# Casts ahead of the power, stores on GpSimd's queue, and the eleventh pair turned by DMA, in a fused windowed-attention and gMLP kernel

## The chip, the core and the metric

The kernel runs on one core of a Trainium2 chip. A core has five engines that run at the same time, each with its own list of instructions in a fixed order, and they wait for each other on semaphores: TensorE (PE in the profile; matmuls, with its weight loads shown as PEld), VectorE (DVE), ScalarE (ACT), GpSimd (POOL) and SyncE (SP, which here only issues transfers). Transfers are moved by 16 DMA engines. An engine that issues a transfer puts it on its own queue and goes on; the transfer lands some microseconds later. The metric is the time of one execution on the device in microseconds; lower is better.

## The reference

There are 4 batches, 8 heads, 768 tokens and 64 channels per head. Attention sees a window of 128 tokens and 4 sink tokens at the start; a gated MLP block (gMLP) follows, with a matrix that mixes tokens.

```python
def _attn_ref(q, k, v, n_sink, window):
    scores = np.matmul(q, k.transpose(0, 1, 3, 2)) / np.sqrt(D)
    rel = pos[:, None] - pos[None, :]
    keep = (pos[None, :] < n_sink) | ((rel >= 0) & (rel < window))
    scores = np.where(keep, scores, -1e9)
    a = np.exp(scores - np.max(scores, axis=-1, keepdims=True))
    a = a / (np.sum(a, axis=-1, keepdims=True) + 1e-09)
    return np.matmul(a, v)

def _moe_ref(x, w_in, g_ln, w_sg, b_sg, w_out):
    h = gelu_tanh(x @ w_in)
    u, v = h[..., :512], h[..., 512:]
    v_n = (v - mean(v)) / np.sqrt(var(v) + 1e-06) * g_ln
    v_s = np.einsum('ts,bsd->btd', w_sg, v_n) + b_sg[None, :, None]
    return x + (u * v_s) @ w_out

# x is the attention's output, all heads side by side: 4 x 768 x 512
```

## The kernel before

**Pairs and batches.** The work is cut into 16 pairs of heads, numbered 0 to 15, four to a batch (batch b holds pairs 4b to 4b + 3). The 768 tokens are 6 tiles of 128. Keys and queries of a pair are loaded in f32 (`load`, L91), cast to bf16 (`cast`, L102, on GpSimd for all but the first pair), and turned so that channels lie on the partitions. There are two ways to turn them. `columns` (L217) does six 128x128 transposes on TensorE into a PSUM bank, which ScalarE or VectorE copies out. `columns_by_dma` (L230) issues one transposing DMA for k and one for q on SyncE's queue. The two ways need different orders of the tokens, so the load differs too: up to pair `FIRST` - 1 a partition takes six neighbouring tokens, a run of 1,536 bytes; from `FIRST` on (L89; `in_rows`) it takes one token of each tile, in rows of 256 bytes. v is always loaded in rows. `FIRST` is 11, so pairs 11 to 15 are turned by DMA.

**One pair.** `score` (L253) computes the scores in three groups of up to 1,024 columns; ScalarE takes their exponentials (L283). `keep_band` (L285) zeroes what lies outside the window: group 0 on VectorE with a mask (L292), groups 1 and 2 on GpSimd with two selects each (L300, L302). `values` (L309) multiplies with v in two halves and VectorE divides by the sums (L334, L335). `turn_x` (L339, TensorE) or `turn_x_by_dma` (L354, SyncE's queue) turns the result for the MLP.

**One batch of the MLP.** `hidden` (L587) has 14 units on TensorE: six for v (L372, L379), each followed by a gelu on ScalarE and statistics on VectorE (L383, L384), and eight for u (L391). After the eighth unit `inverse_root` (L402) forms 1/sqrt(var + 1e-6): VectorE adds (L406, tile w) and GpSimd takes the power (L407, tile y). VectorE then normalises six tiles (L413, tile vn). `spatial` (L417) mixes the tokens in eight groups of six matmuls (L423), each closed by two instructions of VectorE (L426, L429). `project` (L449) makes one tile of 128 output rows: four matmuls (L455), then either VectorE adds x (L465), or, with `by_act`, a fifth matmul adds x (L458) and ScalarE copies (L463); then the tile is stored (L467). Spatial groups and projections wait in a list, `fillers`, and are run between the steps of the next batch's attention.

**The order is written out by hand** in `ORDER` (L719) and `INSIDE` (L714: steps put behind a unit of `hidden`), and each engine's list follows it. The words: `S n g` scores, `m n g` masks, `A0 n`, `A1 n` the two halves of the values, `ck`, `cq`, `cv n` casts on GpSimd, `KA`, `QA` turn k or q with ScalarE's copy, `QV` with VectorE's, `TD n` turn k and q by DMA, `XV n`, `XD n` turn x with VectorE's copy or by DMA, `L n` load k and q of pair n and v of pair n - 1, `F c` run c fillers, `B b` the hidden layer of batch b. SyncE's queue holds loads, turns by DMA and most stores, and an instruction that waits there holds all behind it.

**Buffers that make waits.** A loaded tile of each of k, q and v has three buffers (`loads`, L55), the cast tile two (L107), so a cast of pair n waits until pair n - 2 has been turned; turned tiles have three (L222). PSUM has four single banks in turn for all but scores (`bank`, L211), and two double banks for scores.

At the end (L783 on) the last pair's values, the last hidden layer and its spatial groups and projections run. Its six tiles are stored as `rows` (L606) and `project_last` (L431), which stores one half from SyncE and one from ScalarE. Before that, `count_good` (L479) counts on GpSimd whether all sums are in range; if not, a general path runs, which these inputs do not take.

Of the kernel before, what the change touches and what calls it, by code (L numbers as in the profile page):

```python
# [18 lines left out]
def kernel(  # L19
# [14 lines left out]
    nc = tc.nc  # L34
    V, G, A = nc.vector, nc.gpsimd, nc.scalar

    B, H, S, Dh = q.shape
# [6 lines left out]
    HP = H // 2  # L44
# [3 lines left out]
    HT = NT // 2  # L48
# [37 lines left out]

        nc.sync.dma_start(out=gates[:, i, :], in_=behind)

    FIRST = 3 * HP - 1  # L89

    def load(n, which, eng=None, in_rows=False):  # L91
        b, hp = divmod(n, HP)
        src = dict(k=k, q=q, v=v)[which]
        dst = loads.tile([128, 2, NT, 64], F32, name=which + "_sb")
        order = "h (t p) d -> p h t d" if which == "v" or in_rows else "h (p t) d -> p h t d"
        (eng or nc.sync).dma_start(
            out=dst, in_=src[b, 2 * hp:2 * hp + 2].rearrange(order, t=NT))
        raw[n, which] = dst
# [12 lines left out]
    def load_all(n):  # L111

        for which, m in (("k", n), ("q", n), ("v", n - 1)):
            if m < NP:
                load(m, which, in_rows=m >= FIRST)

# [94 lines left out]
    def bank(shape, dtype, name):  # L211
        return ps_m.tile(shape, dtype, name=name, tag="m")
# [162 lines left out]
    def hidden_v(b, j):  # L375
        if (b, j) not in hvs:
            open_v(b, j)
        h_ps, c = hvs.pop((b, j)), KD - 1
        nc.tensor.matmul(h_ps, xT[b][:, c, 128 * j:128 * (j + 1)],  # L379
                         w_in_sb[:, c, DF:], start=False, stop=True)  # L380
        A.activation(out=v_alls[b][:, j, :], in_=h_ps, func=AF.Gelu_apprx_tanh)  # L381
        st = small.tile([128, 6], F32, name="st")
        V.bn_stats(out=st, in_=v_alls[b][:, j, :])  # L383
        V.bn_aggr(out=mvs[b][:, j, :], in_=st)  # L384

    def hidden_u(b, f, n):
        if f == 0 and n == 0:
            uTs[b] = work.tile([128, KU, S], BF16, name="uT", bufs=1)
        h_ps = bank([128, 512], F32, "hu")
        for c in range(KD):  # L390
            nc.tensor.matmul(h_ps[:, 0:NH], w_in_sb[:, c, 128 * f:128 * (f + 1)],  # L391
                             xT[b][:, c, NH * n:NH * (n + 1)],
                             start=(c == 0), stop=(c == KD - 1))
        A.activation(out=uTs[b][:, f, NH * n:NH * (n + 1)],  # L394
                     in_=h_ps[:, 0:NH], func=AF.Gelu_apprx_tanh)
# [6 lines left out]
    def inverse_root(b):  # L402

        w = small.tile([128, NT], F32, name="w", bufs=2)
        y = small.tile([128, NT], F32, name="y", bufs=2)
        V.tensor_scalar(out=w, in0=mvs[b][:, :, 1], scalar1=1e-6, scalar2=None, op0=ALU.add)  # L406
        G.tensor_tensor(out=y, in0=w, in1=minus_half, op=ALU.pow)  # L407
        rstds[b] = y

    def normalise(b, j):  # L410
        if j == 0:
            vns[b] = work.tile([128, NT, DF], BF16, name="vn", bufs=1)
        V.tensor_scalar(out=vns[b][:, j, :], in0=v_alls[b][:, j, :],  # L413
                        scalar1=mvs[b][:, j, 0:1], scalar2=rstds[b][:, j:j + 1],
                        op0=ALU.subtract, op1=ALU.mult)

    def spatial(b, f, n):  # L417
        if f == 0 and n == 0:
            gTs[b] = work.tile([128, KU, S], BF16, name="gT", bufs=1)
        cols = slice(NH * n, NH * (n + 1))  # L420
        vs = bank([128, 512], F32, "vs")
        for si in range(NT):
            nc.tensor.matmul(vs[:, 0:NH], vns[b][:, si, 128 * f:128 * (f + 1)],  # L423
                             wsgT[:, si, cols], start=(si == 0), stop=(si == NT - 1))
        gv = small.tile([128, NH], BF16, name="gv")
        V.scalar_tensor_tensor(  # L426
            out=gv, in0=vs[:, 0:NH], scalar=g_sb[:, f:f + 1], in1=b_bc[:, cols],
            op0=ALU.mult, op1=ALU.add)
        V.tensor_mul(gTs[b][:, f, cols], gv, uTs[b][:, f, cols])  # L429
# [19 lines left out]
    def project(b, t, by_act, ends=None, store=nc.sync):  # L449

        rows = slice(128 * t, 128 * (t + 1))
        o_ps = bank([128, 512], F32, "o_ps")
        o_sb = small.tile([128, DM], F32, name="o_sb", bufs=6)
        for c in range(KU):
            nc.tensor.matmul(o_ps, gTs[b][:, c, rows], w_out_sb[:, c, :],  # L455
                             start=(c == 0), stop=(c == KU - 1 and not by_act))
        if by_act:
            nc.tensor.matmul(o_ps.rearrange("p (h d) -> p h d", h=HP), iden, x_sb[b][:, :, t, :],  # L458
                             start=False, stop=True)

        def end():
            if by_act:
                A.copy(o_sb, o_ps)  # L463
            else:
                V.tensor_add(o_sb.rearrange("p (h d) -> p h d", h=HP),  # L465
                             o_ps.rearrange("p (h d) -> p h d", h=HP), x_sb[b][:, :, t, :])
            store.dma_start(out=out[b, rows, :], in_=o_sb)  # L467

        if ends is None:
            end()  # L470
        else:
            ends.append(end)
# [34 lines left out]
    def general():  # L507
# [15 lines left out]
        for b in range(B):  # L523
            begin_x(b)
            for hp in range(HP):
                n = HP * b + hp
                for which in "kqv":
                    load(n, which)
                for which in "kqv":
                    cast(n, which, V)  # L530
                columns(n, "k", A)
                columns(n, "q", V)
                for i in range(NT):
                    for l in range(2):
                        stable(n, i, l, m[min(i, 2)], low[:, min(i, 2), :])
                turn_x(n, V)
            hidden(b, {})
            fill(len(fillers))
# [41 lines left out]
    fillers = []  # L580
# [6 lines left out]
    def hidden(b, between):  # L587
        units = [lambda j=j: hidden_v(b, j) for j in range(NT)]
        units += [lambda f=f, n=n: hidden_u(b, f, n) for n in range(2) for f in range(KU)]
        after = {NT + 1: [lambda: inverse_root(b)]}  # L590
        for j in range(NT):
            after.setdefault(NT + 1 + j, []).append(lambda j=j: normalise(b, j))
        for i, unit in enumerate(units):
            unit()
            for step in after.get(i, []) + between.get(i, []):
                step()
        gate = [[lambda f=f, n=n: spatial(b, f, n) for f in range(KU)] for n in range(2)]
        if b < B - 1:
            fillers.extend(gate[0] + gate[1])
            by_act = (1,)  # L600
            order = (0, 2, 4, 1, 3, 5) if b < B - 2 else (1, 0, 2, 3, 4, 5)
            fillers.extend(lambda ends=None, t=t: project(b, t, t in by_act, ends) for t in order)
            return


        rows = [lambda t=t: project(b, t, t in (0, 4), store=nc.sync if t else G)  # L606
                for t in range(NT - 1)]
        fillers.extend(gate[0] + [gate[1][0], rows[0], gate[1][1], gate[1][2], rows[1],
                                  gate[1][3]] + rows[2:])
        fillers.append(lambda: project_last(b, NT - 1))  # L610
# [85 lines left out]
    for j in range(3):  # L696
# [15 lines left out]

    LAST = NT + 2 * KU - 1
    INSIDE = {  # L714
        1: {1: "A0 8", 3: "A1 8", 5: "KA 9", 6: "L 12", 7: "QA 9",
            9: "XD 8, ck 11, cq 11, TD 11, L 13", LAST: "cv 10, S 9 0 1, F 1, QV 10, F 1"},
        2: {1: "A0 12", 3: "A1 12", 6: "L 15, L 16", 9: "XD 12", LAST: "S 13 0 1, F 2"},
    }
    ORDER = """  # L719
        S 4 0 1, W 3 4 5, m 4 0 1, F 1, KA 5, QV 5, F 1, S 4 2, m 4 2, ck 6, cq 6, cv 5, F 1,  # L720
        L 8, S 5 0 1, A0 4, m 5 0 1, F 1, KA 6, S 5 2, m 5 2, A1 4, F 1, QA 6,
        ck 7, cq 7, cv 6, F 1, XV 4,
        L 9, S 6 0 1, A0 5, m 6 0 1, F 1, KA 7, S 6 2, m 6 2, A1 5, F 1, QA 7,
        ck 8, cq 8, cv 7, F 1, XV 5,
# [1 line left out]
        ck 9, cq 9, cv 8, F 1, XV 6,  # L726
        L 11, S 8 0 1, A0 7, m 8 1, D, S 8 2, m 8 2, A1 7, E, m 8 0, ck 10, cq 10, cv 9,
        O 1 0, O 1 1, XV 7, O 1 2, B 1,
        m 9 0 1, F 1, KA 10, F 1, S 9 2, m 9 2, ck 12, cq 12, TD 12, F 1,
        S 10 0 1, A0 9, m 10 0 1, F 1, S 10 2, m 10 2, A1 9, XD 9, L 14,  # L730
        F 1, cv 11, ck 13, cq 13, TD 13, F 1,
        S 11 0 1, A0 10, m 11 0 1, F 1, S 11 2, m 11 2, A1 10, F 1, cv 12, ck 14, cq 14, TD 14,
        F 1, XV 10,
        S 12 0 1, A0 11, m 12 1, F 1, S 12 2, m 12 2, A1 11, F 1, m 12 0, cv 13, F 1,
        O 2 0, O 2 1, XV 11, O 2 2, B 2,
        ck 15, m 13 0 1, cq 15, F 2, S 13 2, m 13 2, TD 15, cv 14, F 1,
        S 14 0 1, A0 13, m 14 0 1, F 1, S 14 2, m 14 2, A1 13, XD 13, F 1, cv 15, F 1,
        S 15 0 1, A0 14, m 15 0 1, F 1, S 15 2, m 15 2, A1 14, XD 14, F 1, G, F 1
    """
# [1 line left out]
    ends = []  # L741
# [97 lines left out]
```

## Time and profile before

| | us |
|---|---|
| median of 3 runs | 164.02 (163.75 to 164.38) |
| the profiled execution | 164.03 |
| its span, from the first instruction to the last | 162.0 |

| engine | busy us | share of the span |
|---|---|---|
| TensorE, matmuls | 150.3 | 93% |
| VectorE | 128.8 | 79% |
| ScalarE | 103.0 | 64% |
| GpSimd | 87.2 | 54% |

The span is some 2 us shorter than the execution's time; a difference between two kernels can be read in either. The granted clock of TensorE is full (1.00) in all stretches that are shown. Times in the profile's rows are microseconds from the start of the span. A row of a timeline has the start, the length, the engine, the line, the operation, what it writes and reads, and how many instructions are merged; in brackets stands idle time ahead of it and what ended it. Lengths of matmuls are modelled and overlap, so the step from one start to the next is what a group of them costs. A few records of matmuls are missing, so that a group of four may read x3.

### The profile page before, as it was taken

To read this page: it belongs to the slowest core of one execution; us is meant where nothing else is said; L and a number is where in the kernel's file an instruction comes from. 1 tells how busy PE (TensorE), PEld (TensorE's weight loads), DVE (VectorE), ACT (ScalarE), POOL (GpSimd) and SP (SyncE) were. 2 spreads that over 40 slices of the span, in tenths; PEclk is the share of its full clock that TensorE was granted. 3 is DMA by queue.
4 is the path that set the end of the run, shared out by engine and by line. 5 is a ranking of instruction groups with operands and counts; after the bars stand their busy time and mean duration, and the time that the engine had idled before them with its cause. 6 is when DMAs were issued, how large, how long until landed. Compare 5 with 4: busy or idle time off the path is not lost.

```text
span 162.0 us, 4332 instructions
## 1 busy us (share of the span) xinstructions
PE 150.3 (93%) x1713; PEld 89.9 (55%) x1731; DVE 128.8 (79%) x279; ACT 103.0 (64%) x139; POOL 87.2 (54%) x121
## 2 busy tenths in 40 slices
PE   2999999999999999999899999999999899999940
PEld 2546574566667675565556655565566445555420
DVE  6786985966899995796999994969999957797820
ACT  3179978789777699788865576679659157401020
POOL 6567680434899989708449997031997221101000
PEclk9999999999999999999999999999999999999995
DMA  4999979999999999999897999999626420050352
GB/s 129 339 337 264 210 103 272 222 254 318 305 232 321 260 304 314 234 256 171 182 249 175 154 220 126 304 236 200 178 52 53 134 109 4 0 194 0 129 202 75
DMA packets 65090, 31.68 MB, mean 196 GB/s; under 512 B 53829, under 2 KB 62041, under 8 KB 65065
## 3 DMA queue, kind: packets, MB, share of 16 engines
q1 hardware_dynamic: 61616, 27.80, 74.8%
q0 software_dynamic: 3024, 3.03, 11.0%
q10 hardware_dynamic: 424, 0.53, 1.0%
q8 instruction: 15, 0.25, 0.7%
q14 instruction: 11, 0.08, 0.1%
HBM read 24.81 MB, written 6.29 MB: 192 GB/s over the span
## 4 chain that ended last, share of the span: by engine, by line
PE 45%; DVE 23%; issue 11%; POOL 10%; DMA 3%; ACT 3%; SPq 1%; POOLq 0%; ACTq 0%; DVEq 0%
PE vs L423 9%; PE hu L391 7%; PE o_ps L455 6%; PE hv L372 5%; DVE gv L426 4%; DVE gT L429 4%; DVE vn L413 4%; PE sc L269 3%; PE av L326 3%; DMA q_sb<-in_q_dram 3%; ACT ex L283 2%; DVE x L335 2%; POOL ex L300 2%; POOL ex L302 2%; PE kps L221 2%
## 5 line engine op out<-in xcount | busy, mean ns | idle before, releaser
L283 ACT ACTIVATE ex<-sc 128x1024 bf16<-128x1024 f32 x48 | 47.5, 1024 | 15.3 <-PE sc L269 6.4
L423 PE MATMUL vs<-wsgT,vn 128*128 128x384 bf16 x192 | 35.3, 326 | 0.5 <-DVE qT L227 0.4
L423 PEld LDWEIGHTS <-vn 128*128 128x128 bf16 x192 | 17.9, 98 | 11.3 <-issue 0.5
L300 POOL TENSOR_SCALAR_AFFINE_SELECT ex<-ex 128x512 bf16<-128x512 bf16 x24 | 18.6, 773 | 10.4 <-ACT ex L283 10.4
L455 PE MATMUL o_ps<-w_out_sb,gT 128*128 128x512 bf16 x83 | 22.2, 379 | 0.9 <-DVE x L335 0.4
L391 PE MATMUL hu<-xT,w_in_sb 128*128 128x384 bf16 x128 | 22.4, 326 | 0.0
L426 DVE SCALAR_TENSOR_TENSOR gv<-vs,g_sb,b_bc 128x384 bf16<-128x384 f32 x32 | 19.5, 610 | 2.1 <-PE vs L423 1.4
L381 ACT ACTIVATE v_all<-hv 128x512 f32<-128x512 f32 x24 | 13.3, 599 | 9.6 <-PE hv L379 8.4
L383 DVE BATCH_NORM_STATS2 st<-v_all 128x6 f32<-128x512 f32 x24 | 16.1, 670 | 3.5 <-ACT v_all L381 3.5
L335 DVE TENSOR_TENSOR x<-av,rcps 128x384 bf16<-128x384 f32 x32 | 17.8, 557 | 1.1
L372 PE MATMUL hv<-w_in_sb,xT 128*128 128x512 bf16 x68 | 18.4, 379 | 0.3
L394 ACT ACTIVATE uT<-hu 128x384 bf16<-128x384 f32 x32 | 15.7, 493 | 4.3 <-PE hu L391 3.8
L108 POOL CAST k_bf<-k_sb 128x768 bf16<-128x768 f32 x15 | 12.7, 845 | 10.3 <-DMA k_sb<-in_k_dram 10.3
L413 DVE TENSOR_SCALAR vn<-v_all,mv,y 128x512 bf16<-128x512 f32 x24 | 13.3, 619 | 5.9 <-POOL y L407 5.9
L429 DVE TENSOR_TENSOR gT<-gv,uT 128x384 bf16<-128x384 bf16 x32 | 15.5, 484 | 1.9
L108 POOL CAST q_bf<-q_sb 128x768 bf16<-128x768 f32 x15 | 14.7, 981 | 3.3 <-DMA q_sb<-in_q_dram 2.4
L391 PEld LDWEIGHTS <-w_in_sb 128*128 128x128 bf16 x128 | 12.1, 98 | 7.7
L269 PE MATMUL sc<-qT,kT 64*128 64x256 bf16 (+2 forms) x384 | 16.0, 256 | 0.4
L407 POOL TENSOR_TENSOR y<-w,minus_half 128x6 f32<-128x6 f32 x4 | 5.4, 1345 | 20.0 <-DVE w L406 20.0
L326 PE MATMUL av<-v_sb,ex 128*128 128x65 bf16 x352 | 16.1, 194 | 0.0
L326 PEld LDWEIGHTS <-ex 128*128 128x128 bf16 x352 | 13.0, 97 | 4.9 <-issue 1.7
L105 POOL CAST v_sb<-v_sb 128x768 bf16<-128x768 f32 x16 | 13.7, 855 | 3.4 <-DMA v_sb<-in_v_dram 3.3
(89 smaller groups left out, 216.5 us busy)
## 6 DMA issues: line engine op xcount, KB each, us to landing
k_sb<-in_k_dram SPq DMA_DIRECT2D x16, 384.0 KB, 6.9
v_sb<-in_v_dram SPq DMA_DIRECT2D x16, 384.0 KB, 6.4
q_sb<-in_q_dram SPq DMA_DIRECT2D x15, 384.0 KB, 6.9
out_dram<-o_sb SPq DMA_DIRECT2D x22, 256.0 KB, 2.6
wsg_sb<-in_moe_w_sg_dram POOLq DMA_DIRECT2D x2, 576.0 KB, 11.4
w_in_sb<-in_moe_w_in_dram POOLq DMA_DIRECT2D x2, 256.0 KB, 5.8
w_in_sb<-in_moe_w_in_dram POOLq DMA_DIRECT2D x1, 512.0 KB, 6.7
w_out_sb<-in_moe_w_out_dram POOLq DMA_DIRECT2D x1, 512.0 KB, 9.5
```

Source lines behind the costliest of these rows:

```text
L108: eng.tensor_copy(dst.rearrange("p t (h d) -> p h t d", h=2), src)
L269: nc.tensor.matmul(sc[part, 512 * l + w:512 * l + w + n_q], kT[rows, 128 * j + wide * a:128 * j + wide * (a + 1)], qT[rows, 128 * j:128 * ...
L283: A.activation(out=exps[n][:, g, :], in_=sc, func=AF.Exp, scale=scale)
L300: eng.affine_select(out=diag, in_=diag, compare_op=ALU.is_ge, fill=0.0, base=0, pattern=[[0, 2], [0, 2], [1, 128]], channel_multiplier=-1)
L326: nc.tensor.matmul(av[:, m, l, :], probs(j, l, half), v_sb[:, l, j, :], start=first, stop=False)
L335: V.tensor_mul(x_sb[b][:, hp, HT * c:HT * (c + 1), :].rearrange("p i (l d) -> p i l d", l=2), av[:, :, :, 0:64], rcp.to_broadcast([128, HT ...
L372: nc.tensor.matmul(hvs[b, j], xT[b][:, c, 128 * j:128 * (j + 1)], w_in_sb[:, c, DF:], start=(c == 0), stop=False)
L391: nc.tensor.matmul(h_ps[:, 0:NH], w_in_sb[:, c, 128 * f:128 * (f + 1)], xT[b][:, c, NH * n:NH * (n + 1)], start=(c == 0), stop=(c == KD - 1))
L423: nc.tensor.matmul(vs[:, 0:NH], vns[b][:, si, 128 * f:128 * (f + 1)], wsgT[:, si, cols], start=(si == 0), stop=(si == NT - 1))
L426: V.scalar_tensor_tensor(out=gv, in0=vs[:, 0:NH], scalar=g_sb[:, f:f + 1], in1=b_bc[:, cols], op0=ALU.mult, op1=ALU.add)
L429: V.tensor_mul(gTs[b][:, f, cols], gv, uTs[b][:, f, cols])
L455: nc.tensor.matmul(o_ps, gTs[b][:, c, rows], w_out_sb[:, c, :], start=(c == 0), stop=(c == KU - 1 and not by_act))
```

## The change

- `FIRST` is 10 instead of 11: k and q of pair 10 are loaded in rows and turned by DMA (`TD 10`); `KA 10` and `QV 10` are gone.
- Behind unit 6 of the hidden layer of batch 1 now stand `TD 10, L 12, ck 11, cq 11`; the casts stood behind unit 9, so that on GpSimd they came after the power (L407), which is issued behind unit 7. `cv 10` moves from the end of that hidden layer to behind the masks of pair 9.
- `L 13`, `L 14`, `L 15` and `L 16` stand behind `TD 12`, `TD 13`, `TD 14` and `TD 15`. Before, they were issued behind units 9 and 6 of the hidden layers of batches 1 and 2 or ahead of the turn of the pair before.
- The casts and turns of pairs 13 and 14 stand later: those of 13 behind the masks of pair 11, those of 14 behind the masks of pair 12. `cq 15` stands ahead of the masks of pair 13.
- `KA 6` stands behind `S 5 2`.
- Tile 5 of batch 1 is added to x on TensorE and copied by ScalarE (`by_act`) instead of added by VectorE.
- Five of the six stores of batch 2 (tiles 0, 2, 3, 4, 5) are issued from GpSimd's queue instead of SyncE's. In batch 3 GpSimd stores tile 3 instead of tile 0.

```diff
-    FIRST = 3 * HP - 1
+    FIRST = 3 * HP - 2
...
-            by_act = (1,)
+            by_act = (1, 5) if b == B - 3 else (1,)
             order = (0, 2, 4, 1, 3, 5) if b < B - 2 else (1, 0, 2, 3, 4, 5)
-            fillers.extend(lambda ends=None, t=t: project(b, t, t in by_act, ends) for t in order)
+
+            by_pool = () if b < B - 2 else order[1:]
+            fillers.extend(lambda ends=None, t=t: project(b, t, t in by_act, ends,
+                                                          G if t in by_pool else nc.sync)
+                           for t in order)
...
-        rows = [lambda t=t: project(b, t, t in (0, 4), store=nc.sync if t else G)
+        rows = [lambda t=t: project(b, t, t in (0, 4), store=G if t == HT else nc.sync)
...
-        1: {1: "A0 8", 3: "A1 8", 5: "KA 9", 6: "L 12", 7: "QA 9",
-            9: "XD 8, ck 11, cq 11, TD 11, L 13", LAST: "cv 10, S 9 0 1, F 1, QV 10, F 1"},
-        2: {1: "A0 12", 3: "A1 12", 6: "L 15, L 16", 9: "XD 12", LAST: "S 13 0 1, F 2"},
+        1: {1: "A0 8", 3: "A1 8", 5: "KA 9", 6: "TD 10, L 12, ck 11, cq 11", 7: "QA 9",
+            9: "XD 8, TD 11", LAST: "S 9 0 1, F 2"},
+        2: {1: "A0 12", 3: "A1 12", 9: "XD 12", LAST: "S 13 0 1, F 2"},
...
-        L 8, S 5 0 1, A0 4, m 5 0 1, F 1, KA 6, S 5 2, m 5 2, A1 4, F 1, QA 6,
+        L 8, S 5 0 1, A0 4, m 5 0 1, F 1, S 5 2, m 5 2, KA 6, A1 4, F 1, QA 6,
...
-        m 9 0 1, F 1, KA 10, F 1, S 9 2, m 9 2, ck 12, cq 12, TD 12, F 1,
-        S 10 0 1, A0 9, m 10 0 1, F 1, S 10 2, m 10 2, A1 9, XD 9, L 14,
-        F 1, cv 11, ck 13, cq 13, TD 13, F 1,
-        S 11 0 1, A0 10, m 11 0 1, F 1, S 11 2, m 11 2, A1 10, F 1, cv 12, ck 14, cq 14, TD 14,
+        m 9 0 1, F 2, S 9 2, m 9 2, ck 12, cq 12, TD 12, L 13, cv 10, F 1,
+        S 10 0 1, A0 9, m 10 0 1, F 1, S 10 2, m 10 2, A1 9, XD 9,
+        F 1, cv 11, F 1,
+        S 11 0 1, A0 10, m 11 0 1, F 1, S 11 2, m 11 2, A1 10, F 1, ck 13, cq 13, TD 13, L 14, cv 12,
         F 1, XV 10,
-        S 12 0 1, A0 11, m 12 1, F 1, S 12 2, m 12 2, A1 11, F 1, m 12 0, cv 13, F 1,
+        S 12 0 1, A0 11, m 12 1, F 1, S 12 2, m 12 2, A1 11, F 1, m 12 0, ck 14, cq 14, TD 14, L 15, cv 13, F 1,
         O 2 0, O 2 1, XV 11, O 2 2, B 2,
-        ck 15, m 13 0 1, cq 15, F 2, S 13 2, m 13 2, TD 15, cv 14, F 1,
+        ck 15, cq 15, TD 15, L 16, m 13 0 1, F 2, S 13 2, m 13 2, cv 14, F 1,
```

## The prediction

> **What bounds the kernel now.** I read the page first (busy shares), then who waited for whom on TensorE, then TensorE's own timeline around the eleventh pair.
>
> ```profile
> span 162.0 us, 4332 instructions
> ## 1 busy us (share of the span) xinstructions
> PE 150.3 (93%) x1713; PEld 89.9 (55%) x1731; DVE 128.8 (79%) x279; ACT 103.0 (64%) x139; POOL 87.2 (54%) x121
> ```
> ```profile
> PE o_ps L455 <- DVE x L335: 0.4, 1, 0.4
> PE vs L423 <- DVE qT L227: 0.4, 1, 0.4
> ```
>
> TensorE is busy for 93% of the span, and these two waits are all that the view of waits lists for it after its warm-up, apart from one of 0.2 us in the start. So the time is the length of TensorE's list of work. Whatever leaves that list is gained, whatever makes TensorE wait is lost, and what happens on another engine counts only when TensorE comes to need it. Here is the list where the eleventh pair (number 10 in the code) is turned:
>
> ```profile
> 75.88 0.61 PE L269 MATMUL sc<-qT,kT 64*128 64x256 bf16 x8
> 76.42 1.04 PE L455 MATMUL o_ps<-w_out_sb,gT 128*128 128x512 bf16 x3
> 77.30 0.50 PE L221 MATMUL qps<-iden,q_bf 128*128 128x128 bf16 x6
> 77.63 1.03 PE L455 MATMUL o_ps<-w_out_sb,gT 128*128 128x512 bf16 x4
> 78.50 1.14 PE L423 MATMUL vs<-wsgT,vn 128*128 128x384 bf16 x6
> 79.70 0.50 PE L221 MATMUL kps<-iden,k_bf 128*128 128x128 bf16 x6
> 80.56 1.14 PE L423 MATMUL vs<-wsgT,vn 128*128 128x384 bf16 x6 [0.37 <-DVE qT L227]
> 81.63 0.36 PE L269 MATMUL sc<-qT,kT 64*32 64x256 bf16 x16
> ```
>
> The columns are start, length and instruction. Lengths of matmuls overlap, so I take steps from start to start.
>
> **The change part by part.** *Pair 10 by DMA.* The two groups of six transposes (L221) leave TensorE, and their copies leave VectorE and ScalarE. From the scores at 75.88 to the next at 81.63 are 5.75 us. Without the groups there remain 0.54 (scores), 0.88 and 0.87 (two projections) and two spatial groups of 1.07 each (80.56 to 81.63): 4.43 us. That is a gain of 1.3 us. The groups alone would be 0.33 each (77.30 to 77.63), 0.66 together; the rest is the wait for the copy of qT. So the bounds are 0.66 and 1.3. I take 1.3, because the spatial sums need only the normalised rows (vn), and those come earlier:
>
> ```profile
> 73.34 1.34 POOL L407 TENSOR_TENSOR y<-w,minus_half 128x6 f32<-128x6 f32 x1 [5.34 <-DVE w L406]
> 74.66 0.81 POOL L108 CAST k_bf<-k_sb 128x768 bf16<-128x768 f32 x1
> 75.42 1.02 POOL L108 CAST q_bf<-q_sb 128x768 bf16<-128x768 f32 x1
> 76.39 1.02 POOL L105 CAST v_sb<-v_sb 128x768 bf16<-128x768 f32 x1
> ```
> ```profile
> 74.00:80.00 6.00, 4.33 (x6) 1.00 0.90 157
> 108.00:113.00 5.00, 3.31 (x6) 1.00 1.37 219
> 139.00:143.00 4.00, 2.40 (x6) 1.00 0.03 12
> ```
>
> The second view is VectorE's time on line 413 in three stretches, six instructions each. Beside the three casts above six take 4.33 us; in batch 2, with one such cast beside them, 3.31; in batch 3, with GpSimd idle, 2.40. *The casts ahead of the power* move two of the three in front of y, and cv 10 goes behind the masks. So vn should end 74.7 + 2.4 to 3.3 = 77.1 to 78.0, and TensorE asks for the sixth only at about 78.17 + 5/6 of 1.07 = 79.1.
>
> What the power waits for is new: in GpSimd's order it now stands behind cq 11, which needs the buffer that QA 9 reads:
>
> ```profile
> 71.55 0.50 PE L221 MATMUL qps<-iden,q_bf 128*128 128x128 bf16 x6
> ```
>
> That ends at 72.05; a cast of 0.81 to 1.02 ends at 72.9 to 73.1, and y starts at 73.34 anyway. I cost it at nothing. The cover is 0.3 us here and 1.1 to 2.0 us ahead of the sixth vn. The Trainium skill, page "SBUF — State Buffer", section "Who interferes with whom", says that a VectorE instruction with at most one SBUF input outside the 2-port modes does not contend with GpSimd. The casts now run beside statistics (L383) of that kind, so by that rule they keep 0.81 us, the power is not late, and the rival below that makes it late gets less; no run here shows it yet.
>
> *Rows instead of runs for k and q of pair 10* (FIRST one lower). The two transfers are 2 x 384 KB. A stretch with mostly long runs and one with short rows show what the DMA engines then move (last column, GB/s):
>
> ```profile
> 50.00:51.20 1.20, 1.20 (x21) 0.82 (x18) 1.20 (x2) 1.13 (x2) 1.20 (x2) 1.00 1.06 359
> 105.00:111.00 6.00, 6.00 (x41) 3.35 (x41) 4.38 (x12) 4.82 (x10) 2.10 (x2) 1.00 1.30 224
> ```
>
> 786 kB take 2.2 us at 359 and 3.5 at 224, so all that is queued behind lands some 1.3 us later, and the two new turns add themselves. Behind them on SyncE's queue stand L 12's three loads, XD 8 and TD 11. Their first user is the scores of pair 11, ahead of which TensorE still has all of pair 10's scores and values and four more spatial groups to do, so I cost this at nothing; without that cover it is 1.3 us.
>
> *Loads timed anew.* L 13, L 14 and L 15 now stand behind the turn of the pair before them, which waits for GpSimd's casts, and XD 9 stands behind L 13. Durations on that queue:
>
> ```profile
> 85.34 1.22 SPq L235 DMA_TRANSPOSE kT<-k_bf  x1
> 86.66 1.22 SPq L235 DMA_TRANSPOSE qT<-q_bf  x1
> 87.98 1.25 SPq L356 DMA_TRANSPOSE xT<-x  x1
> 89.28 1.43 SPq L96 DMA_DIRECT2D k_sb<-in_k_dram  x1
> 90.77 0.70 SPq L96 DMA_DIRECT2D q_sb<-in_q_dram  x1
> 91.51 1.67 SPq L96 DMA_DIRECT2D v_sb<-in_v_dram  x1
> 93.35 2.51 SPq L235 DMA_TRANSPOSE kT<-k_bf  x1
> ```
> ```profile
> 97.96 1.24 PE L372 MATMUL hv<-w_in_sb,xT 128*128 128x512 bf16 x5
> ```
> ```profile
> DMA to landing us min/median/max: 4.1/4.5/5.0
> ```
>
> The turn of pair 12 begins 3.7 us after S 9 2 (81.63 to 85.34: exponential, masks, cast k). S 9 2 comes at 80.3 now, so the turn at 84.0; its two issues take 2.6 and L 13's three 4.1 (89.28 to 93.35), so XD 9 is issued at 90.7 and lands, by the row for xT, 4.1 to 5.0 us later: 94.8 to 95.7. The hidden layer that reads it comes at 97.96 - 1.3 = 96.6. A margin of 1 to 2 us, where before it was 97.96 - (87.98 + 5.0) = 5. Landing like a plain load in a full queue (6.9, below) it would be 1.0 late. I charge 0.2 us for this and the other late users, between 0 and 2.
>
> *One projection of batch 1 to ScalarE* adds a matmul of 128x512 to TensorE's list: 0.87 / 4 = +0.2 us. VectorE loses an addition there, besides the copy of qT and about 0.9 us on vn of batch 2 (3.31 to 2.40) if its casts wait for their loads. That matters where VectorE was late for TensorE:
>
> ```profile
> 126.32 1.04 PE L455 MATMUL o_ps<-w_out_sb,gT 128*128 128x512 bf16 x4 [0.44 <-DVE x L335]
> ```
>
> I take 0.4 for it; 0 if VectorE is no earlier.
>
> *Stores.* Five of batch 2 go to GpSimd's queue: two before the counting, three after the last power, where it has nothing else to do, so they cost nothing; if they held the last power, TensorE would wait for vn of batch 3 by as much. In the last batch tile 3 goes to GpSimd and tile 0 to SyncE. The end:
>
> ```profile
> 155.53 1.12 SPq L467 DMA_DIRECT2D out_dram<-o_sb  x1
> ...
> 156.30 0.38 ACTq L447 DMA_DIRECT2D out_dram<-o_last  x1
> 156.74 0.54 SPq L447 DMA_DIRECT2D out_dram<-o_last  x1
> ```
>
> SyncE's last store stands behind one that took 1.12 us to issue. With one less ahead it can go earlier, but the end gains at most the 0.44 to ScalarE's last. I take 0.2, between 0 and 0.4. The Trainium skill speaks against this part: "SBUF — State Buffer", section "A bandwidth-pool intuition that's wrong", has a store from GpSimd's queue taking 3.1 us instead of 0.62 beside a VectorE copy, as its descriptors cannot be written; by that this term would be 0 and the sum 162.7. No run here shows it. KA 6 behind S 5 2 is the same work in another order, covered by those scores: nothing.
>
> Sum from the profiled execution's 164.03 (the median shown is 164.02): - 1.3 + 0.2 - 0.4 - 0.2 + 0.2 = 162.5.
>
> **The rivals.** *The loads come late (slower).* One ring: turn of q, then k and q of the next load, then casts, then the next turn. One lap is 1.3 (86.66 to 87.98) + 1.5 (k's issue, 89.28 to 90.77) + the landing L + 1.0 (cast) = 3.8 + L. cq 12 ends at about 85.3 (84.0 + 1.3, where its own turn follows it); three laps and XD 9 later cq 15 ends at 98.0 + 3 L, and it now stands ahead of the masks that A0 13 needs:
>
> ```profile
> 116.02 0.48 PE L326 MATMUL av<-v_sb,ex 128*128 128x65 bf16 x10
> ```
> ```profile
> 90.77 4.40 DMA q_sb<-in_q_dram
> ```
> ```profile
> q_sb<-in_q_dram SPq DMA_DIRECT2D x15, 384.0 KB, 6.9
> ```
>
> A0 13 comes at 116.02 - 1.1 = 114.9, less 0.8 for the first mask: it holds up to L = 5.4. Each us more costs 3. The chain of waits shows 4.40 in this very stage, the page's median is 6.9 (most of those loads met a full queue). At 5.9 the gain is gone, at 6.9 the time is 167.1.
>
> *Only the bare work goes (no change by measure).* The waits return at other places because VectorE stays as late: - 0.66 + 0.2 = 163.6. For it: VectorE is busy 79% of the span, more than any engine but TensorE, and both waits above name it. Against it: between the second power and the hidden layer of batch 2 it sheds more than TensorE does (a copy, and up to 1.9 of the 4.33 us on vn).
>
> *The power is late.* If q of pair 11 lands after 72.1, cq 11 and y slide, and past the 1.1 to 2.0 us of cover TensorE stands before the spatial sums. 2 us late would leave 164.03 - 0.5 = 163.5. Against it: in its old place at 75.42 the cast of q 11 waited for nothing, so the load had landed some time before; how long, this trace's rows do not say.
>
> **How the numbers follow.** Forecast 0.64, late loads 0.17, bare work 0.13, late power 0.06. Below 163.2 is faster by more than 0.5%, which is about what a measurement can tell: the forecast gives 0.64 and the late loads with a small L 0.04, so 0.68. Above 164.8 lies the rest of the late loads, 0.13; between them the bare work and the late power, 0.19. The range: all terms at their good ends give 162.5 - 0.2 - 0.2 = 162.1, and I go 0.8 below it, to 161.3, for waits that hide in the steps of matmuls and may go too (78.50 to 79.70 is 0.13 longer than 1.07, and no wait is shown there). The upper end takes L = 6.1: 164.6.
>
> **What would show it.** Right: no L221 of pair 10 on TensorE; six vn after the second power in 2.4 to 3.3 us; S 9 2 at 80.3; the hidden layer of batch 2 at 96.6; no wait at the projection after A0 15. Wrong: a wait of TensorE for xT at the hidden layer of batch 2, GpSimd idle for q_sb ahead of cq 14 or cq 15 with ScalarE's exponentials done, y of batch 1 starting later than 73.4, or of batch 2 behind cv 13.

## The result and the profile after

| | before | changed |
|---|---|---|
| median of the runs | 164.19 us (6 runs) | 162.64 us (161.87 to 165.96, 6 runs) |
| ratio to before | 1 | 0.9885, 95% interval 0.9853 to 0.9917 |
| ratio, the same kernel in a second set of runs | 1 | 0.9898, interval 0.9849 to 0.9946 |
| profiled execution, span | 164.03, 162.0 us | 161.53, 159.7 us |

By the ratio the change makes the kernel 1.2% faster, some 1.9 us. Every kernel here has now and then an execution that is some per cent longer, which counts in the medians of this document but not in its ratios; the first profiled execution of the change (165.42 us) was such a one, so the lines here are of another profiled execution of the same kernel, run repeat. What the first one lost is shown at the end. The page of the second and its view of waits (engine, line, tile, who was waited for, and us in total, times, longest):

```profile
span 159.7 us, 4312 instructions
## 1 busy us (share of the span) xinstructions
PE 149.1 (93%) x1702; PEld 89.4 (56%) x1720; DVE 126.1 (79%) x277; ACT 102.8 (64%) x139; POOL 89.3 (56%) x126
```
```profile
...
PE xps L343 <- DVE x L335: 0.2, 1, 0.2
```

TensorE is still the bound, with 1.2 us less work. The two waits of 0.4 us are gone, and a new one of 0.2 us stands at `XV 10`, for VectorE's x; the lines left out are waits in the kernel's first 40 us. TensorE's timeline around pair 10, and at the two hidden layers behind it:

```profile
75.81 0.61 PE L269 MATMUL sc<-qT,kT 64*128 64x256 bf16 x8
76.35 1.90 PE L455 MATMUL o_ps<-w_out_sb,gT 128*128 128x512 bf16 x7
78.09 2.11 PE L423 MATMUL vs<-wsgT,vn 128*128 128x384 bf16 x12
80.13 0.36 PE L269 MATMUL sc<-qT,kT 64*32 64x256 bf16 x16
```
```profile
96.69 1.46 PE L372 MATMUL hv<-w_in_sb,xT 128*128 128x512 bf16 x6
...
126.12 1.03 PE L455 MATMUL o_ps<-w_out_sb,gT 128*128 128x512 bf16 x4
126.98 0.81 PE L372 MATMUL hv<-w_in_sb,xT 128*128 128x512 bf16 x3
```

Between the scores at 75.81 and S 9 2 at 80.13 there are 4.32 us instead of 5.75, and no L221 stands between them. The hidden layer of batch 2 comes at 96.69. VectorE's time on vn (line 413; columns: window, its length, busy time and count, clock, DMA share, GB/s):

```profile
74.00:80.00 6.00, 2.83 (x6) 1.00 1.34 226
106.00:112.00 6.00, 3.33 (x6) 1.00 1.22 227
136.00:142.00 6.00, 2.88 (x6) 1.00 0.02 8
```

The group of batch 1 takes 2.83 us instead of 4.33; that of batch 2 is as long as before (3.31). In batch 3 GpSimd is idle, and there six take 2.88, before and after. The prediction has 2.40 for them: its window began at 139.00, after the first of the six, which begins at 138.52. In batch 0 of the kernel before, GpSimd idle too, six take 2.83. So 2.83 us is all that the casts could leave, and each cast that runs beside the six adds some 0.5 us: 2.83 with none, 3.31 with one, 3.82 with two (run casts_behind), 4.33 with three. GpSimd around the second power, and where the loads come latest:

```profile
70.46 0.83 POOL L108 CAST k_bf<-k_sb 128x768 bf16<-128x768 f32 x1 [2.55 <-PE kps L221]
72.10 0.83 POOL L108 CAST q_bf<-q_sb 128x768 bf16<-128x768 f32 x1 [0.81 <-PE qps L221]
73.26 1.34 POOL L407 TENSOR_TENSOR y<-w,minus_half 128x6 f32<-128x6 f32 x1 [0.34 <-DVE w L406]
...
110.11 0.89 POOL L108 CAST k_bf<-k_sb 128x768 bf16<-128x768 f32 x1 [2.20 <-DMA k_sb<-in_k_dram]
111.93 1.24 POOL L108 CAST q_bf<-q_sb 128x768 bf16<-128x768 f32 x1 [0.93 <-DMA q_sb<-in_q_dram]
113.12 0.77 POOL L300 TENSOR_SCALAR_AFFINE_SELECT ex<-ex 128x512 bf16<-128x512 bf16 x1
```

The power starts at 73.26, having waited 0.34 us for w alone: it was not late. cq 15 did wait for its load, the masks of pair 13 stand right behind it without a gap, and they start at 113.12.

Starts of such rows give a table of stages for every run below, in us: A from the scores of S 9 to S 9 2, B from there to the hidden layer of batch 2, C from S 13 to the hidden layer of batch 3, D from there to the end of the span. Between B and C lie 11.76 or 11.77 us in every run. A row is one profiled execution, that of the change its second.

| run | A | B | C | D | ratio to before, interval |
|---|---|---|---|---|---|
| before | 5.75 | 16.33 | 18.87 | 33.41 | 1 |
| the change | 4.32 | 16.56 | 18.53 | 32.72 | 0.9898 (0.9849 to 0.9946) |
| no_turn10 | 4.99 | 16.57 | 18.47 | 33.08 | 0.9925 (0.9889 to 0.9961) |
| casts_behind | 4.33 | 17.54 | 18.48 | 33.03 | 0.9945 (0.9906 to 0.9985) |
| loads_early | 4.32 | 17.13 | 19.21 | 33.21 | 0.9939 (0.9906 to 0.9972) |
| casts_loads | 4.32 | 18.18 | 19.20 | 33.27 | 0.9983 (0.9954 to 1.0011) |
| turn10_only | 4.46 | 20.16 | 18.87 | 33.13 | 1.0053 (1.0012 to 1.0094) |
| loads_only | 5.75 | 17.16 | 19.35 | 33.50 | 1.0054 (1.0026 to 1.0082) |
| stores_sp | 4.32 | 16.56 | 18.48 | 33.06 | 0.9867 (0.9839 to 0.9895) |
| act_one | 4.32 | 16.56 | 18.25 | 32.98 | 0.9865 (0.9806 to 0.9923) |
| ka6_back | 4.32 | 16.57 | 19.96 | 32.98 | 0.985 (0.982 to 0.9881) |
| three_parts | 4.33 | 16.57 | 18.66 | 33.02 | 0.9901 (0.9863 to 0.9939) |
| turn9 | 5.56 | 17.54 | 19.61 | 34.00 | 1.0049 (1.0019 to 1.0079) |

How far can such a row be trusted? The change's first profile has A 4.33, B 16.56, C 18.47 and D 33.01. In the five runs whose edit touches neither the turn of pair 10 nor its casts nor the loads, A and B agree with that within 0.01. So a few tenths in A and B are the edit's, also where the ratios' intervals overlap, as those of no_turn10, casts_behind and loads_early do with the change's. D is looser: from the hidden layer of batch 3 to TensorE's last group of matmuls it is 27.0 us in the kernel before and in both profiles of the change; what differs is the time behind that group.

From before to the change the stages give - 1.43 + 0.23 - 0.34 - 0.69, and - 0.07 ahead of A: 2.3 us less span in this pair of executions, of which the ratio keeps 1.9. With the D of the first profile it would be 0.3 less.

### The profile page after: what moved, and what is told of

Read it like the earlier page. It is cut to its first block, busy times and chain, and to the rows that moved or that the text cites. A ratio compares the mean times of both kernels' runs of the same rounds, so it can differ in the third digit from the quotient of the medians.

```text
span 163.6 us, 4330 instructions
## 1 busy us (share of the span) xinstructions
PE 150.2 (92%) x1720; PEld 88.5 (54%) x1720; DVE 129.0 (79%) x277; ACT 102.9 (63%) x139; POOL 89.1 (54%) x126
## 4 chain that ended last, share of the span: by engine, by line
PE 63%; DVE 18%; DMA 12%; issue 2%; POOL 1%; SPq 1%; ACT 0%; POOLq 0%; DVEq 0%
PE vs L423 13%; PE o_ps L455 12%; PE hu L391 11%; DMA q_sb<-in_q_dram 8%; PE hv L372 7%; DVE gT L429 6%; PE sc L269 5%; PE av L326 4%; DMA w_in_sb<-in_moe_w_in_dram 3%; DVE gv L426 3%; PE hv L379 2%; DVE x L335 2%; DVE vsink L162 2%; PE xps L343 2%; DVE qT L227 1%
## 5 line engine op out<-in xcount | busy, mean ns | idle before, releaser
L300 POOL TENSOR_SCALAR_AFFINE_SELECT ex<-ex 128x512 bf16<-128x512 bf16 x24 | 17.6, 733 | 10.2 <-ACT ex L283 10.0
L429 DVE TENSOR_TENSOR gT<-gv,uT 128x384 bf16<-128x384 bf16 x32 | 19.9, 622 | 1.9
L108 POOL CAST q_bf<-q_sb 128x768 bf16<-128x768 f32 x15 | 13.9, 925 | 6.3 <-DMA q_sb<-in_q_dram 4.8
L413 DVE TENSOR_SCALAR vn<-v_all,mv,y 128x512 bf16<-128x512 f32 x24 | 11.9, 564 | 6.4 <-POOL y L407 6.4
L302 POOL TENSOR_SCALAR_AFFINE_SELECT ex<-ex 128x512 bf16<-128x512 bf16 (+1 forms) x24 | 14.0, 582 | 0.0
```

Of the source, the lines that this page charges most:

```text
L108: eng.tensor_copy(dst.rearrange("p t (h d) -> p h t d", h=2), src)
L300: eng.affine_select(out=diag, in_=diag, compare_op=ALU.is_ge, fill=0.0, base=0, pattern=[[0, 2], [0, 2], [1, 128]], channel_multiplier=-1)
```

## The experiments

They ran in three sets, each on one chip and beside the kernel before: repeat, no_turn10, casts_behind and loads_early; turn10_only, stores_sp, act_one and ka6_back; casts_loads, loads_only, three_parts and turn9.

**The change itself again, repeat** (no edit), for a second profile and the second ratio above.

> The changed kernel once more, unaltered, as the measure for the other three runs. If the result stands, its ratio to the kernel before is 0.985 to 0.992. In its profile the theory of TensorE's list expects the stage from the scores of pair 9 (groups 0, 1) to the next scores in 4.3 to 4.4 us (5.75 before), the hidden layer of batch 2 reached 1.1 to 1.3 us earlier than before, and no wait at the projection after A0 15. It also tells whether VectorE's product gT (L429) of the first spatial groups takes some 0.4 us or the 3.35 us that the changed kernel's first profile shows once.

The median was 162.58 us.

**no_turn10: pair 10 back on TensorE, all else as in the change.**

```diff
-    FIRST = 3 * HP - 2
+    FIRST = 3 * HP - 1
...
-6: "TD 10, L 12, ck 11, cq 11",  ...  LAST: "S 9 0 1, F 2"
+6: "L 12, ck 11, cq 11",  ...  LAST: "S 9 0 1, F 1, QV 10, F 1"
...
-        m 9 0 1, F 2, S 9 2
+        m 9 0 1, F 1, KA 10, F 1, S 9 2
```

> Pair 10 goes back to TensorE (KA 10, QV 10, runs of 1,536 bytes); all else of the change stays. Theory of TensorE's list: 0.66 us of transposes come back, and up to 0.7 of waits for a bank of PSUM with them, so 0.7 to 1.4 us slower than the changed kernel, ratio to the kernel before 0.992 to 0.997. Rival (the gain is VectorE's undisturbed vn, from the casts ahead of the power): most of the gain stays, under 0.5 us slower than the changed kernel.

The median was 163.33 us, the span 160.4, and A is 4.99: of the 1.43 us only 0.67 came back, the two groups of transposes and nothing else. The wait for the copy of qT did not return, with vn at 2.83 us; with vn at 4.33 (run loads_only below) A stays at 5.75. So either edit takes that wait away; the 1.3 of the sum was two things, 0.66 of work that only the DMA removes, and some 0.7 of a wait that the casts would have removed as well.

**casts_behind: the casts of pair 11 behind the power again.**

```diff
-6: "TD 10, L 12, ck 11, cq 11",  ...  9: "XD 8, TD 11",
+6: "TD 10, L 12",  ...  9: "XD 8, ck 11, cq 11, TD 11",
```

> ck 11 and cq 11 go back behind unit 9, so behind the power; all else of the change stays. Theory of TensorE's list: vn takes about 4 us instead of 2.8 and ends about when TensorE asks for its last tile, so 0 to 0.4 us slower than the changed kernel. Rival (the gain is VectorE's undisturbed vn): at least 1 us of the gain is lost, ratio to the kernel before 0.994 or more.

The median was 163.85 us, and B is 0.98 longer, the rival's mechanism. Of this kernel, VectorE's vn, VectorE's quotient for the second half of pair 10, and the turn on TensorE that reads it:

```profile
74.00:80.00 6.00, 3.82 (x6) 1.00 1.29 229
```
```profile
91.82 0.56 DVE L335 TENSOR_TENSOR x<-av,rcps 128x384 bf16<-128x384 f32 x1
```
```profile
92.43 0.34 PE L343 MATMUL xps<-iden,x 128*128 128x128 bf16 x3 [0.92 <-DVE x L335]
```

And that quotient in the change:

```profile
91.08 0.56 DVE L335 TENSOR_TENSOR x<-av,rcps 128x384 bf16<-128x384 f32 x1
```

vn is 3.82 - 2.83 = 0.99 us longer, and B is 0.98 us longer. Counted from S 9 2, which comes 0.24 earlier in this execution, the quotient is 0.98 later too. Between vn and the quotient VectorE has no idle time worth a bracket in this kernel: what vn loses beside the casts is paid some fifteen microseconds later at `XV 10`. Once pair 10's transposes are gone, VectorE is what TensorE runs up against in this stage, and the casts are what makes room on it.

**loads_early: the loads L 13 to L 16 at their old places.**

```diff
-9: "XD 8, TD 11", ...  TD 12, L 13, ...  TD 13, L 14, ...  TD 14, L 15, ...  TD 15, L 16,
+9: "XD 8, TD 11, L 13", ...  TD 12, ...  XD 9, L 14, ...  2: {..., 6: "L 15, L 16",
```

> L 13 to L 16 go back to their places of before (behind TD 11, behind XD 9, and behind unit 6 of the hidden layer of batch 2); casts and turns stay as in the change. Theory of TensorE's list: no user waits for these loads in the changed kernel, so within 0.2 us of it. Rival (late loads cost something that the wait view does not list): 0.3 to 1 us faster than the changed kernel.

The median was 163.81 us; B is 0.57 longer and C 0.68. Two of its waits on TensorE:

```profile
PE o_ps L455 <- DVE x L335: 0.5, 1, 0.5
PE sc L269 <- DMA qT<-q_bf: 0.5, 1, 0.5
```

The scores of pair 12 wait for their turned q: L 13's issues stand ahead of that turn, which goes out at 85.74 instead of 83.76. The wait behind A0 15 is back, and both casts of pair 15 now run beside vn of batch 2, which takes 3.82 us. The new places of the loads, which I had charged with a loss of 0.2, gain 1.25 us in B and C; between the two ratios lie 0.7 us.

**turn10_only: the turn of pair 10 alone, put into the kernel before.**

```diff
-    FIRST = 3 * HP - 1
+    FIRST = 3 * HP - 2
...
-6: "L 12",  ...  LAST: "cv 10, S 9 0 1, F 1, QV 10, F 1"
+6: "TD 10, L 12",  ...  LAST: "cv 10, S 9 0 1, F 2"
...
-        m 9 0 1, F 1, KA 10, F 1, S 9 2
+        m 9 0 1, F 2, S 9 2
```

> The kernel before with one edit: pair 10 is loaded in rows and turned by DMA (TD 10); casts, loads and stores stay where they were. Theory (TensorE's list, with both waits named): the two groups of transposes leave TensorE, 0.66 us, and the wait for the copy of qT with them, so 0.7 to 1.4 faster than before, ratio 0.991 to 0.996; six vn still beside the casts, 3.8 to 4.5 us, because cast v of pair 10 still comes behind the power. From S 9 2 on the old timing of the loads holds, so the hidden layer of batch 2 may come less early than in the change. Rival (VectorE's lateness only moves): 0.66 or less, ratio 0.996 or above, and a wait at a spatial group <- DVE vn appears near 78 to 80.

Both theories missed. At its place the turn does what was expected, A is 1.29 shorter; but in this execution B is 3.83 us longer, and by the ratio the kernel is 0.5% slower than before. Waits on TensorE, then SyncE's queue ahead of the turn of pair 12, then TensorE's busy time and granted clock (the number behind the count) us by us:

```profile
PE sc L269 <- DMA qT<-q_bf: 1.1, 1, 1.1
PE xps L343 <- DVE x L335: 1.1, 1, 1.1
```
```profile
82.58 0.57 SPq L96 DMA_DIRECT2D k_sb<-in_k_dram  x1
83.21 0.70 SPq L96 DMA_DIRECT2D q_sb<-in_q_dram  x1
83.95 1.75 SPq L96 DMA_DIRECT2D v_sb<-in_v_dram  x1
85.79 2.17 SPq L467 DMA_DIRECT2D out_dram<-o_sb  x2
88.13 1.30 SPq L235 DMA_TRANSPOSE kT<-k_bf  x1
```
```profile
95.00:96.00 1.00, 1.00 (x10) 0.65 1.23 266
96.00:97.00 1.00, 1.00 (x26) 0.50 1.35 232
97.00:98.00 1.00, 1.00 (x30) 0.50 1.34 213
98.00:99.00 1.00, 0.88 (x4) 0.64 1.38 222
```

L 13's three issues and two stores stand ahead of the turn of pair 12, which goes out at 88.13; in the change, where only the two stores stand there, it goes out at 83.76 although S 9 2 is at the same time. Two waits of 1.1 us follow within 3 us, and then the granted clock falls to 0.50: 0.35 + 0.50 + 0.50 + 0.36 = 1.7 us of work lost. 1.1 + 1.1 + 1.7 is the 3.8. The fall of the clock was seen in this one execution. By the ratio the kernel loses 0.9 us, where this execution has 2.1 us more span than the kernel before.

**casts_loads: both undone together** (the edits of the third and fourth run; the casts of pairs 13 and 14 stay late).

> The change with two parts undone at once: the casts of pair 11 stand behind the power and the loads L 13 to L 16 at their old places; the casts and turns of pairs 13 and 14 keep the new places. Each alone cost 1.0 and 1.2 us. Theory A (the two hurt each other: late casts of pair 11 make all of SyncE's queue late, and the early loads make it later still): from S 9 2 to the hidden layer of batch 2 19 to 20.2 us (20.16 with the turn of pair 10 alone, 16.56 in the change), TensorE waits 1 us or more for the turned q of pair 12, the time is 3 to 4 above the change, at or above that of before. Rival B (they add): 18.0 to 18.3 us in that stage, 2.0 to 2.3 above the change, ratio to before 0.997 to 1.002; then the rest of the loss of the turn alone belongs to the casts of pairs 13 and 14, which stood ahead of the masks.

B is 18.18: 0.98 + 0.57 = 1.55 from the single edits, 1.62 together. They add, as the second theory had it. It went on to give the rest of the loss of the turn alone to the places of the casts of pairs 13 and 14; of those 2.0 us (20.16 - 18.18) the clock explains 1.7, since here it stays at 1.00 with waits of 0.9 and 0.6. For the places of those casts that leaves no more than some tenths.

**loads_only: the new timing of loads, casts and turns of pairs 13 to 15 alone, in the kernel before** (pair 10 on TensorE, ck 11 and cq 11 behind the power, stores and tile 5 as before).

> The kernel before with the new places of the loads L 13 to L 16 and of the casts and turns of pairs 13 to 15 alone; pair 10 is turned on TensorE and the casts of pair 11 stand behind the power. Theory: from the hidden layer of batch 2 on this is what takes the wait at the projection behind A0 15 away, so S 13 to the hidden layer of batch 3 takes 18.2 to 18.5 us instead of 18.87, and the stage of pair 10 keeps its 5.75: 0.3 to 0.7 faster than before, ratio 0.996 to 0.998. Rival (the old timing only hurts when TensorE comes earlier): no change, ratio 0.998 to 1.002. Second rival (the loads come late, as the prediction feared): a wait for the hidden layer of batch 2, ratio above 1.002.

It is 0.5% slower than before, against both the gain and the no change that were expected. Two waits for VectorE are in its list:

```profile
PE xps L343 <- DVE x L335: 0.8, 1, 0.8
PE o_ps L455 <- DVE x L335: 0.7, 1, 0.7
```

Neither is for a load, so the second rival's mechanism isn't it either. The first stands at `XV 10`, and two instructions of VectorE account for it:

```profile
90.31 1.13 DVE L292 TENSOR_TENSOR ex<-ex,mask 128x1024 bf16<-128x1024 bf16 x1
92.01 0.73 DVE L429 TENSOR_TENSOR gT<-gv,uT 128x384 bf16<-128x384 bf16 x1
```

In the kernel before they take 0.68 and 0.36, together 0.82 less. Both have two inputs in SBUF; here they run beside GpSimd's selects, in the kernel before beside casts of pair 13, whose new place let the selects come earlier. The second wait, behind A0 15, is even longer than before: the loads alone don't remove it.

**The three small parts,** one by one and then together: stores on their old queues (stores_sp); tile 5 of batch 1 by VectorE (act_one); KA 6 ahead of S 5 2 (ka6_back); all of it (three_parts).

```diff
-                                                          G if t in by_pool else nc.sync)
+                                                          nc.sync)
...
-store=G if t == HT else nc.sync)
+store=nc.sync if t else G)
```

> The change with the stores on their old queues. Theory: the queue of the stores matters at the end alone, so 0 to 0.4 us slower than the change (0.2 charged), ratio to before 0.989 to 0.993, with SyncE's last store issued behind one more, and the span from the hidden layer of batch 3 to the end 33.0 to 33.4. Rival (a store from GpSimd's queue is held up by VectorE): equal to or faster than the change, and in the change's own trace the GpSimd stores take several us to issue.

```diff
-            by_act = (1, 5) if b == B - 3 else (1,)
+            by_act = (1,)
```

> The change with tile 5 of batch 1 added by VectorE again. Theory: TensorE loses a matmul of 128x512, -0.2 us, and VectorE gains an addition of some 0.5 us, which is near S 12; VectorE waits return only if it is late there: between -0.2 and +0.3 against the change, ratio to before 0.987 to 0.992. Rival (the edit is what removes the wait at the projection behind A0 15): that wait of 0.3 to 0.5 is back and the time is 0.3 to 0.5 above the change.

```diff
-        S 5 2, m 5 2, KA 6, A1 4,
+        KA 6, S 5 2, m 5 2, A1 4,
```

> The change with the turn of k of pair 6 ahead of the scores S 5 2 again. Theory: the same work in another order, covered by those scores: within 0.15 us of the change, ratio to before 0.988 to 0.992. Rival (S 5 2 earlier lets ScalarE and GpSimd start earlier, and a hidden wait goes): 0.3 to 0.6 slower than the change, with the loss between 40 and 55 us.

> The change without its three small parts: stores on their old queues, tile 5 of batch 1 added by VectorE, KA 6 ahead of S 5 2. Theory: the turn of pair 10, the casts of pair 11 and the timing of the loads carry the whole gain; the matmul that adds x is 0.25 us of TensorE's list for nothing: 0.2 to 0.3 below the change, the stage from S 13 to the hidden layer of batch 3 18.25 us, ratio to before 0.984 to 0.988. Rival (the stores are worth the 0.2 that was charged): equal to the change.

No ratio of the four can be told from that of the change. With tile 5 back on VectorE, C is 18.25 instead of 18.47 to 18.53 and no wait returns. The added matmul costs 0.21 us of TensorE's list (in the change from 110.74, its start, to 110.95, the next one's). But VectorE's load did not simply grow by an addition: vn of batch 2 is 0.5 us shorter in act_one, as it is in three_parts and turn9, which have tile 5 on VectorE too:

```profile
106.00:113.00 7.00, 2.83 (x6) 1.00 1.13 229
```

The cast of k of pair 15, which runs beside vn in the change, starts only beside its last instruction or behind it there; why its load lands later against TensorE was not taken apart. With the stores back, D is 33.06, inside the 32.72 to 33.27 of the runs with the new queues. All three undone should have been 0.2 to 0.3 faster and were not measurably so (C is 18.66, with a wait of 0.2 for a turned q); that undoing tile 5 makes a faster kernel is seen in one stage of act_one only, not in a ratio. KA 6 shows nothing in the times (median 162.66); the C of 19.96 is that of one execution of 164.28 us, with three waits around A0 15 of 1.0 us in all.

**turn9: pair 9 by DMA too,** with tile 5 on VectorE.

```diff
-    FIRST = 3 * HP - 2
+    FIRST = 3 * HP - 3
...
-5: "KA 9", 6: "TD 10, L 12, ck 11, cq 11", 7: "QA 9",
+6: "TD 10, L 12, ck 11, cq 11",
...
-        ck 9, cq 9, cv 8, F 1, XV 6,
+        ck 9, cq 9, TD 9, cv 8, F 1, XV 6,
```

> One step further: pair 9 is turned by DMA as well (loaded in rows, TD 9 behind cq 9 ahead of the scores of pair 8; KA 9 and QA 9 gone), and tile 5 of batch 1 is added by VectorE. Theory (TensorE's list): two groups of six transposes less, 0.66 us, so 0.6 to 0.8 faster than the change with tile 5 added by VectorE, ratio to before 0.979 to 0.984, the hidden layer of batch 1 with its spatial start 11.8 us instead of 12.46. Rival (SyncE's queue is full there: the loads of pairs 10 and 11 are in flight, each landing 5 to 6 us after its issue): L 11 behind the turn lands later by 2 to 4 us, cq 11 and the power behind it are late, and TensorE waits for vn of batch 1 by 1 us or more, or for the turned q of pair 9: equal to the change or slower.

The hidden layer of batch 1 got the 0.67 us shorter that was expected (11.79 against 12.46 us from its start to S 9), and the kernel is 1.5% slower than the change: the rival was right. GpSimd:

```profile
72.61 0.83 POOL L108 CAST k_bf<-k_sb 128x768 bf16<-128x768 f32 x1 [4.61 <-DMA k_sb<-in_k_dram]
74.49 0.83 POOL L108 CAST q_bf<-q_sb 128x768 bf16<-128x768 f32 x1 [1.05 <-DMA q_sb<-in_q_dram]
75.28 1.34 POOL L407 TENSOR_TENSOR y<-w,minus_half 128x6 f32<-128x6 f32 x1
```

L 11 stands behind the new turn; GpSimd waits for it, and the second power, which stands behind cq 11, starts 2.0 us later than in the change (73.26). A is 5.56: the rival of the late power, which the change itself escaped by 0.34 us.

## Why the prediction was right

It said 162.5 us; the median came out at 162.64, and 162.3 by the ratio. The main mechanism, transposes and a wait leaving TensorE's list, was right. That the sum is so close is in part luck: one term had the right size for another reason, and one is not shown. Point by point:

- *Pair 10 by DMA, - 1.3.* The stage gave 1.43, with S 9 2 at 80.13 (80.3 was said) and the hidden layer of batch 2 at 96.69 (96.6). Splitting it into 0.66 of work and the rest as a wait was right, and the reason for taking the upper bound (vn earlier) too: 2.83 us, between the 2.4 and 3.3 that were named, though the 2.4 was misread from a window that cut the first of the six. What the sum did not say is that the gain is only kept where two other parts are present; alone in the kernel before, the same edit is 0.5% slower.
- *"only bare work goes"*, the rival, has its mechanism: VectorE is next in line. It did not decide because VectorE shed 1.5 us of vn and a copy; the prediction had up to 1.9, by its 2.40. With the casts behind the power it does decide, by 0.98.
- *The power, 0.* Right: y at 73.26, where 73.34 was said. The cast of q 11, at 72.10, ran beside the statistics below and took 0.83 us, where 0.81 was said. The rule cited from the Trainium skill, page "SBUF — State Buffer", section "Who interferes with whom", agrees with this.

```profile
72.09 0.66 DVE L383 BATCH_NORM_STATS2 st<-v_all 128x6 f32<-128x512 f32 x1
```

- *"I charge 0.2 us for this and the other late users"*: the step that failed, though the number came. B is 0.23 longer, as charged, but for another reason: the wait of 0.2 at `XV 10` is for VectorE; no load and no `XD 9` is waited for. And the step looked only at what a later load makes late, not at what it stood in front of. With the loads early the turn of pair 12 is late; moving them is worth 0.57 us in B and 0.68 in C. The term was off by more than its own size, and the sum came out because the gain was hidden in it: without the new places B would have given back 0.57 of the 1.3, and the 0.4 would not have come.
- *The slower rival, late loads.* Its arithmetic was good: for cq 15 it had 98.0 + 3 L, which with the row below makes 113.9, and the cast was done at about 113.1. GpSimd did stand idle for q_sb ahead of cq 15 (0.93 us), but ScalarE's exponential for group 1 of pair 13 was done only at 112.30, so the selects behind the cast came some 0.8 us late. That cost TensorE nothing: they ended at 114.5, and A0 13 came at 114.97 without a wait. The bound was L = 5.4, and L was 5.3, so it escaped by little. The row groups DMA issues between 83 and 115 us; the last number is the median of us from issue to landing:

```profile
q_sb<-in_q_dram SPq DMA_DIRECT2D x3, 384.0 KB, 5.3
```

- *The wait behind A0 15, - 0.4.* Gone, and for one half of the reason that I named. VectorE's list between the power of batch 2 and that place is full, and the profiles sort by what stands at its head:

| runs | vn of batch 2 | additions behind it | wait |
|---|---|---|---|
| before, turn10_only, loads_only | 3.31, 3.31, 3.33 | two | 0.44, 0.45, 0.70 |
| loads_early, casts_loads | 3.82 | one | 0.49, 0.48 |
| the change, no_turn10, casts_behind, stores_sp | 3.33 to 3.34 | one | none |
| act_one, three_parts, turn9 | 2.83 | two | none in the list of waits |

One addition is 0.6 us and one cast beside vn 0.5 us; with either of them off VectorE the wait goes, and with a cast more and an addition less it is back. In the change it was the addition; the 0.9 us of vn did not come, vn stayed at 3.33. (In three_parts the steps show 0.15 us at that place. ka6_back has 3.34, one addition and a wait of 0.55, in the execution of 164.28 us.)

- *One projection to ScalarE, + 0.2.* 0.21.
- *Stores, - 0.2.* Not shown. The step that was named came: SyncE's last store goes out 0.36 us behind the start of TensorE's last group instead of 1.15. The end did not follow it: from that group to the end of the span lie 5.7 to 6.3 us in the profiles with the new queues (7.0 in turn9) and 6.0 to 6.5 in those with the old ones. The Trainium skill, page "SBUF — State Buffer", section "A bandwidth-pool intuition that's wrong", warns of 3.1 us for a transfer from GpSimd's queue beside a VectorE copy. That case did not arise: beside these stores VectorE ran instructions that read PSUM, or nothing, and each store took 0.54 to 0.62 us to issue. Two rows of GpSimd in the change:

```profile
126.98 0.62 POOL L467 DMA_DIRECT2D out_dram<-o_sb  x1 [2.34 <-DVE rcps L334]
...
140.69 1.73 POOL L467 DMA_DIRECT2D out_dram<-o_sb  x3 [3.81 <-DVE o_sb L465]
```

## What to carry to other kernels

Work taken off the bounding engine brings it forward against the next one: ask for each stage behind it which engine or queue is now late, and by how much. A load issued early is not free on a queue that also carries transfers somebody waits for; put it behind them and check that it still lands in time. And price edits together: the same turn by DMA was worth 0.7 us of TensorE's list with its two companions, and without them it cost 0.9 us by the ratio.

## What the runs showed of the hardware

*The granted clock fell after short gaps.* In turn10_only TensorE was idle for 1.05 us, worked 0.34, and was idle for 1.09 until 94.08; between 95 and 96 us the clock was 0.65, then 0.50 for 2 us. In casts_loads, gaps of 0.92 and 0.57 at the same place left it at 1.00, and in turn9 single gaps of 0.75 and 1.04 did too. In the 14 profiles the clock is below full nowhere else between 14 and 156 us. The Trainium skill, page "TensorE: Matmul & The Clock Gate", section "Why this matters for your kernels", says to keep idle gaps under about 3 us; here the fall came behind two of 1.1 us, close together. It was seen once, and no run varied the gaps alone.

*A VectorE instruction can be passed over by a row of GpSimd instructions.* The change's first profiled execution lost its time at 46 to 53 us. VectorE, then GpSimd:

```profile
44.59 3.35 DVE L429 TENSOR_TENSOR gT<-gv,uT 128x384 bf16<-128x384 bf16 x1
```
```profile
44.41 0.63 POOL L300 TENSOR_SCALAR_AFFINE_SELECT ex<-ex 128x512 bf16<-128x512 bf16 x1
44.99 0.41 POOL L302 TENSOR_SCALAR_AFFINE_SELECT ex<-ex 128x256 bf16<-128x256 bf16 x1
45.37 0.81 POOL L108 CAST k_bf<-k_sb 128x768 bf16<-128x768 f32 x1
46.13 0.82 POOL L108 CAST q_bf<-q_sb 128x768 bf16<-128x768 f32 x1
46.91 0.82 POOL L105 CAST v_sb<-v_sb 128x768 bf16<-128x768 f32 x1
```

The product of two tiles in SBUF takes 0.36 us where GpSimd is idle, and here 3.35: it starts during a select and ends with the last of five GpSimd instructions that follow one another without a gap. A second product in the same execution, at 50.13, took 2.06 us beside a select and two casts. TensorE then waited for VectorE three times, 1.4, 0.3 and 1.3 us. That GpSimd's instructions held it is read from these rows; spacing them out was not tried.
